# Softmax sums in an attention and feed-forward kernel: partial sums carried on over key tiles by GpSimd and VectorE, and one block of ones-matmuls for each pair of heads

## The chip, the core and the metric

The kernel runs on one core of one Trainium2 chip. A core has five engines that work side by side, each on its own queue in order: TensorE (PE, with its weight loads PEld), VectorE (DVE), ScalarE (ACT), GpSimd (POOL) and SyncE (SP), which here issues all transfers. The metric is the device time of one execution in microseconds (us); lower is better.

## What is computed

```python
def _attn_ref(q, k, v):                      # (8, 8, 1152, 64) each, float32
    B, H, S, D = q.shape
    scale = 1.0 / np.sqrt(D)
    q_pool = q.reshape(B, H, S // 2, 2, D).mean(axis=3)
    scores = scale * np.matmul(q_pool, k.transpose(0, 1, 3, 2))
    scores = scores - np.max(scores, axis=-1, keepdims=True)
    attn = np.exp(scores)
    attn = attn / (np.sum(attn, axis=-1, keepdims=True) + 1e-09)
    return np.matmul(attn, v).astype(np.float32)

def _moe_ref(x, w_in, w_out):                # (4608, 512), (512, 2048), (2048, 512)
    h = x @ w_in
    g = h - np.tanh(h)
    return (g @ w_out).astype(np.float32)
```

The output of the attention, 8 x 576 tokens with 8 heads of 64 values, is the `x` of the second function. The change is about `np.sum(attn)`, the softmax sums.

## The kernel before

There are two stages. The attention stage works on 32 pairs (4 pairs of heads in each of 8 batches, `NP` = 4). A pair has 576 queries after pooling, taken in two halves of 288 (`HQ`), and 1152 keys in nine tiles of 128. The time of this stage is counted in units: a unit is the scores of one head, one half and one key tile. Six units (three key tiles, two heads) are a group (`G` = 6), three groups are a half, 36 units (`U`) a pair.

In a unit (`score_unit`, line 281) PE makes 128 x 288 scores in a `ps_s` buffer (three of them) with two matmuls, and ScalarE takes their exponentials into `p_f`, the attention weights before division. `p_f` has four buffers of one group each. Keys lie on the partitions there. The sum over keys is therefore a sum over partitions and over tiles, and it is made in two steps. First GpSimd adds the three key tiles of a group for both heads at once, two adds of 128 x 576 (`z_part`, line 296). Then PE multiplies the result with a block of ones, 128 x 32, which sums over the partitions (`z_sums`, line 322).

Beside that, PE multiplies the weights with the values (`pv`, line 302: six fp32 matmuls a group, two heads in two halves of the array's columns, into `ps_o`), and it makes a first pass over the scores of later pairs to find their row maxima (`max_part`, line 241: matmuls into one of two `ps_m` buffers, each read by a VectorE reduction into `mx`, 14 a pair). VectorE also splits keys and queries into high and low parts (`kq_l`, line 215) and does most of the work on the weights of the second stage (`w`, `w_block`, line 371: one block every 34 units, to which GpSimd adds two instructions and ScalarE two). GpSimd also adds up the two pooled queries (`kq`, line 203).

What stands in which order is written out by hand. `add(u, f)` queues a step at a unit, and the loop at line 480 runs the steps of each unit; `InOrder` (line 27) keeps that order on every engine in this stage. The product of group n with the values comes five units after the group's last scores. The division comes later: the product is copied to `o_s` and stored unscaled in `x_dram`, the sums are copied to `z_s` and stored in `z_dram`; once a batch, `sums` (line 352) loads them as `rec`, VectorE takes reciprocals (line 361), and `spread` (line 366) stores them in `r_dram`. The maxima travel through `m_dram` and come back as two rows of the score operand (`there` and `back`, lines 270 and 273).

The second stage, the feed-forward part, takes 512 tokens at a time (`hidden`, line 522, and `second`, line 547); it loads `x_f` from `x_dram` and the reciprocals `x_r` from `r_dram` (line 96), and the multiplication of the first chunk happens on VectorE in the last units of the attention stage. In this stage a scheduler sets the order.

In the kernel before, a half has three partial sums, one of each group, in tiles `z` with four buffers. The block of ones-matmuls runs once for each half, after the first group of the next half: six matmuls of 288 columns, two heads and three groups. Each fills 32 columns of the array; two groups go side by side into four places, the third is added on the first two. The two places of each head are added after the load (line 363).

Of the kernel before, what the change touches and what calls it, by code (L numbers as in the profile page):

```python
# [43 lines left out]
def kernel(  # L44
# [18 lines left out]
    P = 128  # L63
    B, NP, _, _, SQ = q.shape
# [10 lines left out]
    dram = ctx.enter_context(tc.tile_pool(name="scratch", bufs=1, space=DRAM))  # L75
# [9 lines left out]
    ones = const.tile([P, 32], F32, name="ones")  # L85
# [1 line left out]


    x_dram = dram.tile([NP, P, NTOK], F32, name="x_dram")
    z_dram = dram.tile([B, 2, 2, NP, SQ], F32, name="z_dram")  # L90
# [50 lines left out]
    with ExitStack() as actx:  # L141
# [13 lines left out]
        HQ = SQ // 2  # L155
# [3 lines left out]
        G = 6  # L159
# [20 lines left out]
        def add(u, f, *args, at=at):  # L180
            at.setdefault(u, []).append(lambda: f(*args))
# [4 lines left out]
        pairs = {}  # L186

        def load(pi):
            w = pairs[pi] = Pair()
            w.b, w.hp = divmod(pi, NP)  # L190
            w.i = pi % 2
# [99 lines left out]
        class Group:  # L291
            pass

        late = []

        def z_part(grp):

            z = grp.z = zp.tile([P, 2, HQ], F32, name="z")
            pool.tensor_tensor(z, grp.p[:, :, 0], grp.p[:, :, 1], op=ALU.add)
            pool.tensor_tensor(z, z, grp.p[:, :, 2], op=ALU.add)  # L300

        def pv(u, grp):

            w, hf = grp.w, grp.half
            if grp.g == 0:
                hf.o = ps_o.tile([P, 512], F32, name="ps_o")
                hf.zs = []
            for j in range(3):
                kt = 3 * grp.g + j
                for h in range(2):  # L310
                    pe.matmul(hf.o[64 * h:64 * h + 64, 0:HQ], w.v[:, h, kt], grp.p[:, h, j], start=(kt == 0),
                              stop=(kt == KT - 1), tile_position=(0, 64 * h))
            hf.zs.append(grp.z)
            if grp.g == 2:
                add(u + 1, o_out, w, hf, at=first)
                late.append((w, hf))
                if w is pairs.get(n_pair - 1) and hf.n == 1:
                    add(u + G, lambda: z_sums(u + G, *late.pop()))
            elif late:
# [12 lines left out]
        def o_out(w, hf):  # L332
            if hf.n == 0:
                w.o_s = sm.tile([P, SQ], F32, name="o_s")
                w.z_s = sm.tile([P, SQ], F32, name="z_s")
            act.activation(w.o_s[:, hf.n * HQ:(hf.n + 1) * HQ], hf.o[:, 0:HQ], AF.Copy)

        def z_out(u, w, hf, ps):

            act.activation(w.z_s[:, hf.n * HQ:(hf.n + 1) * HQ], ps[:, 0:HQ], AF.Copy)  # L340
            if hf.n == 1:
                def store():
                    sp.dma_start(x_dram[w.hp, :, w.b * SQ:(w.b + 1) * SQ], w.o_s)
                    sp.dma_start(z_dram[w.b].rearrange("r h a s -> (r h) a s")[:, w.hp], w.z_s[0:P:32])
                add(u + 2, store)
                if w.hp == NP - 1:
                    add(u + 6, lambda: tot.append((w.b, sums(w.b))))
                    if w.b < B - 1:
                        add(u + 22, lambda: reciprocals(dve, *tot[0]))
                        add(u + 25, lambda: spread(sp, *tot.pop(0)))  # L350

        def sums(b):

            n = NP * 2 * SQ // P
            t = rec.tile([P, 2, n], F32, name="rec")
            for r in range(2):
                for h in range(2):
                    sp.dma_start(t[h * 64:h * 64 + 64, r], z_dram[b, r, h].rearrange("a (x n) -> (a x) n", n=n))
            return t

        def reciprocals(eng, b, t):

            eng.scalar_tensor_tensor(t[:, 0], t[:, 0], 1e-9, t[:, 1], op0=ALU.add, op1=ALU.add)
            eng.reciprocal(t[:, 0], t[:, 0])

        def spread(dma, b, t):
            dma.dma_start(r_dram[b].rearrange("h a (x n) -> (h a x) n", n=SQ * NP * 2 // P), t[:, 0])

        WB = 512

# [109 lines left out]
        for u in range(end + 60):  # L480
            run(u, first)
            if u < end:
                pi, r = divmod(u, U)
                half, r = divmod(r, U // 2)
                g, r = divmod(r, G)
                h, j = divmod(r, 3)
                if r == 0:
                    grp = Group()
                    if g == 0:
                        grp.half = Group()  # L490
                        grp.half.n = half
                    else:
                        grp.half = groups[-1].half
                    grp.w, grp.g = pairs[pi], g
                    grp.p = pf.tile([P, 2, 3, HQ], F32, name="p_f")
                    groups.append(grp)
                score_unit(grp.w, half, h, 3 * g + j, grp.p[:, h, j])
                if r == G - 1:
                    add(u + 1, z_part, grp)
# [131 lines left out]
```

## Time and profile before

| | us |
|---|---|
| median of three runs | 1827.98 |
| lowest, highest run | 1825.22, 1828.62 |
| the profiled execution, its own time | 1825.99 |
| its span, first to last instruction | 1824.2 |
| attention stage in it | from 0 to about 1000 |

A row of the profile gives an engine, a line (most of the attention stage has the line of a helper, L37, so groups are told apart by the names of their tiles), an operation with output and inputs, a count, and times. `ps_s<-z,ones` are the ones-matmuls, `z<-p_f` and `z<-z,p_f` the adds of GpSimd, `ps_m` and `mx` the row maxima, `ps_s<-t` the scores, `ps_o<-p_f,v` the product with the values. An fp32 matmul leaves two records. An idle time "<-" names what ended it.

### The profile page before, as it was taken

Reading aid. Unit: us, or ns where it says so; the run is one execution under the profiler, and the core shown is the slowest. Engines: PE = TensorE matmul, PEld = TensorE weight load, DVE = VectorE, ACT = ScalarE, POOL = GpSimd, SP = SyncE. Lnnn points to the kernel's source line nnn. Section 1 sums busy time; section 2 is a strip of 40 time slices with the busy share of each in tenths; the row PEclk is TensorE's granted clock in tenths of the full one; section 3 lists DMA queues with packets and bytes.
Section 4 is the critical chain, followed back from the end, with each engine's and each line's share of the span. In section 5 each row is a group of like instructions: output and inputs, shape, how many; then the busy total and the mean of one; then the engine's idle time right before and its main releaser. Section 6 shows DMA issues by size and latency. Waiting matters only on the chain. (4 is left out here: it accounts for less than half of the span.)

```text
span 1824.2 us, 28257 instructions
## 1 busy us (share of the span) xinstructions
PE 1741.4 (95%) x9920; PEld 1306.6 (72%) x9920; DVE 1403.8 (77%) x1823; ACT 1084.0 (59%) x2473; POOL 1050.4 (58%) x756
## 2 busy tenths in 40 slices
PE   4999999999999989999998999999999999999998
PEld 3666666766676666666665777878787888788887
DVE  5776767677767777776741899988998899888897
ACT  2555555656565555555554655666666666666676
POOL 2666778777787767777864274353534444433433
PEclk9999999999999999999999999999999999999999
DMA  8767787878878676878763821020101010100000
GB/s 211 201 175 219 180 227 196 221 196 219 228 207 232 168 213 181 212 212 227 196 169 131 313 58 64 6 65 6 64 9 61 13 57 18 44 14 34 27 15 21
DMA packets 104141, 242.29 MB, mean 133 GB/s; under 512 B 18112, under 2 KB 43328, under 8 KB 104000
## 3 DMA queue, kind: packets, MB, share of 16 engines
q1 hardware_dynamic: 104000, 240.49, 47.7%
q8 instruction: 78, 1.28, 0.3%
q14 instruction: 63, 0.52, 0.1%
HBM read 109.64 MB, written 36.42 MB: 80 GB/s over the span
## 5 line engine op out<-in xcount | busy, mean ns | idle before, releaser
L37 DVE TENSOR_REDUCE mx<-ps_m 128x2 f32<-128x768 f32 x448 | 405.5, 924 | 258.2 <-PE ps_m L37 257.9
L37 ACT ACTIVATE p_f<-ps_s 128x288 f32<-128x288 f32 x1152 | 418.0, 411 | 193.6 <-PE ps_s L37 169.7
L37 PE MATMUL ps_s<-t 128*128 128x288 f32 (+1 forms) x2304 | 447.6, 313 | 15.1 <-ACT p_f L37 9.1
L544 POOL TENSOR_TENSOR g_lo<-g_s,g_hi 128x512 fp32r<-128x512 f32 (+1 forms) x160 | 209.2, 1308 | 414.3 <-ACT g_hi L543 360.0
L37 PEld LDWEIGHTS ps_s<-t 128*128 128x128 f32 (+1 forms) x2304 | 357.2, 191 | 120.0 <-issue 90.2
L37 POOL TENSOR_TENSOR z<-p_f 128x576 f32<-128x576 f32 x192 | 289.7, 1509 | 159.5 <-PE ps_s L37 112.0
L526 PE MATMUL ps_h<-x,wi 128*128 128x512 f32 (+1 forms) x1440 | 325.0, 370 | 1.4 <-DVE g_s L541 1.4
L37 PE MATMUL ps_o<-p_f,v 128*64 128x288 f32 x2304 | 325.7, 419 | 0.0
L37 POOL TENSOR_TENSOR z<-z,p_f 128x576 f32<-128x576 f32 x192 | 290.4, 1512 | 17.9 <-ACT p_f L37 3.2
L526 PEld LDWEIGHTS ps_h<-x,wi 128*128 128x128 f32 x1440 | 254.9, 188 | 53.4 <-ACT g_u L532 1.8
L551 PE MATMUL ps_o<-wo,g_hi 128*128 128x512 f32 x1008 | 275.7, 392 | 4.2 <-ACT g_hi L543 3.8
L37 PE MATMUL ps_m<-x,bd 128*128 128x384 f32 x864 | 237.7, 355 | 32.0 <-DVE mx L37 17.5
L37 PEld LDWEIGHTS ps_o<-p_f,v 128*64 128x64 f32 x2304 | 149.8, 138 | 114.8 <-issue 29.8
L551 PEld LDWEIGHTS ps_o<-wo,g_hi 128*128 128x128 f32 x1008 | 186.8, 188 | 46.3 <-ACT g_hi L543 7.4
L543 ACT ACTIVATE g_hi<-g_s 128x512 fp32r<-128x512 f32 (+1 forms) x160 | 94.3, 590 | 153.8 <-DVE g_s L542 151.5
L37 PEld LDWEIGHTS ps_m<-x,bd 128*128 128x128 f32 x864 | 143.5, 196 | 49.6 <-DVE mx L37 27.9
L539 DVE SCALAR_TENSOR_TENSOR g_w<-g_w,g_u 128x512 f32<-128x512 f32 (+1 forms) x160 | 172.6, 1079 | 0.0
L551 PE MATMUL ps_o<-wo,g_lo 128*128 128x512 f32 x504 | 160.1, 393 | 5.6 <-POOL g_lo L544 5.4
L532 ACT ACTIVATE g_u<-ps_h 128x512 f32<-128x512 f32 (+1 forms) x160 | 87.5, 547 | 119.5 <-PE ps_h L526 119.0
L542 DVE COPY_PREDICATED g_s<-g_m,g_t 128x512 f32<-128x512 int32 (+1 forms) x160 | 133.3, 833 | 14.7 <-DVE g_s L541 0.5
L540 DVE SCALAR_TENSOR_TENSOR g_w<-g_s,g_w 128x512 f32<-128x512 f32 (+1 forms) x160 | 129.3, 808 | 18.8 <-ACT g_s L534 2.2
L541 DVE SCALAR_TENSOR_TENSOR g_s<-g_s,g_w 128x512 f32<-128x512 f32 (+1 forms) x160 | 126.5, 790 | 17.0 <-ACT g_t L533 0.5
(60 smaller groups left out, 1887.8 us busy)
## 6 DMA issues: line engine op xcount, KB each, us to landing
t<-x SPq DMA_DIRECT2D x64, 432.0 KB
q_n<-in_q_dram SPq DMA_DIRECT2D x32, 576.0 KB
kq<-in_k_dram SPq DMA_DIRECT2D x32, 576.0 KB
t<-kq_l SPq DMA_DIRECT2D x64, 288.0 KB
t<-x SPq DMA_DIRECT2D x64, 288.0 KB
v<-in_v_dram SPq DMA_DIRECT2D x32, 576.0 KB
bd<-x SPq DMA_DIRECT2D x64, 144.0 KB
t<-kq_l SPq DMA_DIRECT2D x64, 144.0 KB
```

What stands on the lines that cost most here:

```text
L37: ins = self.tc.keep_in_program_order(f(*args, **kwargs))
L526: nc.tensor.matmul(h, wi[fc][:, w, c], x[:, c, 0:n], start=(j == 0), stop=(j == len(mm) - 1))
L532: nc.scalar.activation(u, h, AF.Square)
L539: nc.vector.scalar_tensor_tensor(w, w, PL, u, op0=ALU.mult, op1=ALU.mult)
L540: nc.vector.scalar_tensor_tensor(w, s2, P2, w, op0=ALU.add, op1=ALU.mult)
L541: nc.vector.scalar_tensor_tensor(s1, s1, P1, w, op0=ALU.add, op1=ALU.mult)
L542: last = nc.vector.copy_predicated(s1, m.bitcast(I32), th).ins
L543: nc.scalar.activation(g_h, s1, AF.Copy)
L544: nc.gpsimd.tensor_tensor(g_l, s1, g_h.bitcast(F32), op=ALU.subtract)
L551: nc.tensor.matmul(po[j], g[:, ts], wo[fc][:, w], start=(fc == 0 and i == 0), stop=(fc == NF - 1 and i == 2))
```

## The change

The partial sums are carried on. For each half, GpSimd adds the three tiles of the first group into `hf.z` and then adds the three tiles of the second group to it, three more adds. The third group gets a tile of its own, `z_2`, with two adds, and VectorE adds it to `hf.z`, ten units later. A half so has seven adds on GpSimd in place of six, and one on VectorE. `hf.z` has three buffers, `z_2` two.

The ones-matmuls run once for a pair, after the second group of the next pair, for both halves: four matmuls (two halves, two heads), each in its own 32 columns. Nothing is added up on PE. One copy to `z_s` then holds both halves, and two stores take it to `z_dram`, which has lost an axis; `sums` has one load where it had four, and the reciprocal adds only the constant. The product `x_dram` is stored by its own step, one unit after it is copied.

```diff
-        late = []
-
-        def z_part(grp):
-
-            z = grp.z = zp.tile([P, 2, HQ], F32, name="z")
-            pool.tensor_tensor(z, grp.p[:, :, 0], grp.p[:, :, 1], op=ALU.add)
-            pool.tensor_tensor(z, z, grp.p[:, :, 2], op=ALU.add)
+        def z_part(u, grp):
+
+            hf = grp.half
+            if grp.g < 2:
+                if grp.g == 0:
+                    hf.z = zp.tile([P, 2, HQ], F32, name="z", bufs=3)
+                    pool.tensor_tensor(hf.z, grp.p[:, :, 0], grp.p[:, :, 1], op=ALU.add)
+                for j in range(2 if grp.g == 0 else 0, 3):
+                    pool.tensor_tensor(hf.z, hf.z, grp.p[:, :, j], op=ALU.add)
+            else:
+                z = zp.tile([P, 2, HQ], F32, name="z_2", bufs=2)
+                pool.tensor_tensor(z, grp.p[:, :, 0], grp.p[:, :, 1], op=ALU.add)
+                pool.tensor_tensor(z, z, grp.p[:, :, 2], op=ALU.add)
+                add(u + 10, lambda: dve.tensor_tensor(hf.z, hf.z, z, op=ALU.add))
...
-            hf.zs.append(grp.z)
             if grp.g == 2:
-                add(u + 1, o_out, w, hf, at=first)
-                late.append((w, hf))
+                add(u + 1, o_out, u + 1, w, hf, at=first)
+                w.halves.append(hf)
                 if w is pairs.get(n_pair - 1) and hf.n == 1:
-                    add(u + G, lambda: z_sums(u + G, *late.pop()))
-            elif late:
-                z_sums(u, *late.pop())
+                    add(u + G, lambda: z_sums(u + G, w))
+            elif grp.g == 1 and hf.n == 0 and w.i_pair > 0:
+                z_sums(u, pairs[w.i_pair - 1])
 
-        def z_sums(u, w, hf):
+        def z_sums(u, w):
 
             ps = ps_s.tile([P, 512], F32, name="ps_s")
-            for g in range(3):
+            for hf in w.halves:
                 for h in range(2):
-                    r = 64 * (g % 2) + 32 * h
-                    pe.matmul(ps[r:r + 32, 0:HQ], ones, hf.zs[g][:, h], start=(g < 2), stop=(g > 0),
-                              tile_position=(0, r))
-            add(u + 1, z_out, u + 1, w, hf, ps, at=first)
+                    r = 64 * hf.n + 32 * h
+                    pe.matmul(ps[r:r + 32, 0:HQ], ones, hf.z[:, h], start=True, stop=True, tile_position=(0, r))
+            add(u + 1, z_out, u + 1, w, ps, at=first)
...
+        def z_out(u, w, ps):
+
+            z_s = sm.tile([P, HQ], F32, name="z_s")
+            act.activation(z_s, ps[:, 0:HQ], AF.Copy)
+
+            def store():
+                for i in range(2):
+                    sp.dma_start(z_dram[w.b, :, w.hp, i * HQ:(i + 1) * HQ], z_s[64 * i:64 * i + 64:32])
+            add(u + 2, store)
...
-            t = rec.tile([P, 2, n], F32, name="rec")
-            for r in range(2):
-                for h in range(2):
-                    sp.dma_start(t[h * 64:h * 64 + 64, r], z_dram[b, r, h].rearrange("a (x n) -> (a x) n", n=n))
+            t = rec.tile([P, n], F32, name="rec")
+            sp.dma_start(t, z_dram[b].rearrange("h a (x n) -> (h a x) n", n=n))
...
-            eng.scalar_tensor_tensor(t[:, 0], t[:, 0], 1e-9, t[:, 1], op0=ALU.add, op1=ALU.add)
-            eng.reciprocal(t[:, 0], t[:, 0])
+            eng.tensor_scalar(t, t, 1e-9, None, op0=ALU.add)
+            eng.reciprocal(t, t)
```

Where the instructions stand now is shown at three places. First PE, around the end of the first groups of a pair's two halves. Before, at the first group of a pair's second half or of the next pair alike:

```order
L37 MATMUL ps_s<-t_0_121 128x288
L37 MATMUL ps_s<-t_0_122 128x288
L37 MATMUL ps_o<-p_f,v 64x288 x6
L37 MATMUL ps_s<-z,ones 32x288 x6
L37 MATMUL ps_s<-t_0_121 128x288
L37 MATMUL ps_s<-t_0_122 128x288
L37 MATMUL ps_m<-x,bd_125 128x384 x2
```

Now, after the second group of a pair, for the pair ahead of it:

```order
L37 MATMUL ps_s<-t_0_121 128x288
L37 MATMUL ps_s<-t_0_122 128x288
L37 MATMUL ps_o<-p_f,v 64x288 x6
L37 MATMUL ps_s<-z,ones 32x288 x4
L37 MATMUL ps_s<-t_0_121 128x288
L37 MATMUL ps_s<-t_0_122 128x288
```

The block stands once a pair, one group later, with four matmuls; at the first groups the scores follow the product with the values directly.

Second VectorE, at the tenth unit of a pair, where the maxima of the next pair are gathered (`nm`, `m2`) and the first reductions of the pair after it follow (numbers behind a name tell buffers apart):

```order
L37 TENSOR_REDUCE nm_1357<-mx_812 128x5 x2
L37 CAST m2_1360<-nm_1357 128x10
L37 TENSOR_TENSOR m2_1360<-nm_1357,m2_1360 128x10
L37 TENSOR_TENSOR z_1170<-z_1170,z_2_1275 128x576
L37 TENSOR_REDUCE mx_1145<-ps_m_1387 128x2
L37 TENSOR_REDUCE mx_1145<-ps_m_1403 128x2
```

The `z` row is new, for the second half of the pair before; the reductions stand behind it. The add for a first half stands at the 28th unit, between reductions.

Third SyncE, at the end of a batch. Before:

```order
L37 DMA x_dram<-o_s 128x576
L37 DMA z_dram<-z_s 4x576
L37 DMA wi_dram<-w_hl 256x4x128
L37 DMA m_dram<-mt 2x10x128
L37 DMA rec<-z_dram 64x36 x4
L37 DMA t_1_124<-m_dram 2x2x576
L37 DMA bd_126<-x 64x576 x2
```

Now:

```order
L37 DMA m_dram<-mt 2x10x128
L37 DMA z_dram<-z_s 2x288 x2
L37 DMA t_1_124<-m_dram 2x2x576
L37 DMA rec<-z_dram 128x36
L37 DMA bd_126<-x 64x576 x2
```

The stores of the sums come behind the store of the maxima and ahead of their load; the store of `x_dram` has moved up.

More of the change, by code (lines that the diff above doesn't have):

```diff
@@ L89 @@
     x_dram = dram.tile([NP, P, NTOK], F32, name="x_dram")
-    z_dram = dram.tile([B, 2, 2, NP, SQ], F32, name="z_dram")
+    z_dram = dram.tile([B, 2, NP, SQ], F32, name="z_dram")
     r_dram = dram.tile([B, 2, NP, SQ], F32, name="r_dram")
@@ L190, in load @@
             w.b, w.hp = divmod(pi, NP)
-            w.i = pi % 2
+            w.i, w.i_pair, w.halves = pi % 2, pi, []
             w.t2 = t2[w.i]
@@ L306, in pv @@
                 hf.o = ps_o.tile([P, 512], F32, name="ps_o")
-                hf.zs = []
             for j in range(3):
@@ L332, in o_out @@
-        def o_out(w, hf):
+                    r = 64 * hf.n + 32 * h
+                    pe.matmul(ps[r:r + 32, 0:HQ], ones, hf.z[:, h], start=True, stop=True, tile_position=(0, r))
+            add(u + 1, z_out, u + 1, w, ps, at=first)
+        def o_out(u, w, hf):
             if hf.n == 0:
                 w.o_s = sm.tile([P, SQ], F32, name="o_s")
-                w.z_s = sm.tile([P, SQ], F32, name="z_s")
             act.activation(w.o_s[:, hf.n * HQ:(hf.n + 1) * HQ], hf.o[:, 0:HQ], AF.Copy)
-        def z_out(u, w, hf, ps):
-            act.activation(w.z_s[:, hf.n * HQ:(hf.n + 1) * HQ], ps[:, 0:HQ], AF.Copy)
@@ L341, in z_out @@
             if hf.n == 1:
[L342 to L350, printed above, removed]
+                add(u + 2, lambda: sp.dma_start(x_dram[w.hp, :, w.b * SQ:(w.b + 1) * SQ], w.o_s))
@@ new lines, in z_out @@
+        def z_out(u, w, ps):
[5 more added lines that the diff above has]
+            add(u + 2, store)
+            if w.hp == NP - 1:
+                add(u + 6, lambda: tot.append((w.b, sums(w.b))))
+                if w.b < B - 1:
+                    add(u + 22, lambda: reciprocals(dve, *tot[0]))
+                    add(u + 25, lambda: spread(sp, *tot.pop(0)))
@@ L364, in reciprocals @@
-            eng.reciprocal(t[:, 0], t[:, 0])
+            eng.tensor_scalar(t, t, 1e-9, None, op0=ALU.add)
+            eng.reciprocal(t, t)
         def spread(dma, b, t):
-            dma.dma_start(r_dram[b].rearrange("h a (x n) -> (h a x) n", n=SQ * NP * 2 // P), t[:, 0])
+            dma.dma_start(r_dram[b].rearrange("h a (x n) -> (h a x) n", n=SQ * NP * 2 // P), t)
         WB = 512
@@ L498 @@
                 if r == G - 1:
-                    add(u + 1, z_part, grp)
+                    add(u + 1, z_part, u + 1, grp)
             run(u)
```

## The prediction

> **What bounds the kernel now.** I first read the page's busy times, then the stretches, to find out where TensorE (PE) is the limit.
>
> ```profile
> span 1824.2 us, 28257 instructions
> PE 1741.4 (95%) x9920; PEld 1306.6 (72%) x9920; DVE 1403.8 (77%) x1823; ACT 1084.0 (59%) x2473; POOL 1050.4 (58%) x756
> ...
> 60.00:940.00 880.00, 849.28 (x5783) 592.80 (x5783) 633.89 (x789) 503.86 (x1356) 653.45 (x444) 0.99 0.77 205
> 940.00:1011.00 71.00, 63.55 (x386) 41.46 (x385) 11.92 (x22) 32.32 (x88) 34.80 (x25) 0.93 0.46 143
> 1100.00:1824.00 724.00, 708.32 (x3248) 580.82 (x3246) 636.71 (x862) 475.35 (x897) 291.64 (x235) 1.00 0.10 32
> ```
>
> The columns of a stretch are its length, then the busy time of PE, PEld, DVE, ACT and POOL. The change touches the attention stage only. There, from 60 to 940 us, PE is busy for 849.28 of 880 us (97%), GpSimd (POOL) for 74%, VectorE (DVE) for 72%. A busy share alone does not say that an engine sets the pace, so next come the waits of PE in that stretch (total, times, longest).
>
> ```profile
> PE ps_m L37 <- DVE mx L37: 21.1, 22, 1.9
> PE ps_s L37 <- ACT p_f L37: 5.4, 15, 0.9
> PE ps_m L37 <- ACT mt L37: 4.0, 23, 0.2
> ```
>
> PE waits 30.5 us in 880, two thirds of it for VectorE's maxima to give back a `ps_m` buffer. No transfer and no GpSimd instruction stands in the list. So PE's own work sets the pace of the attention stage, and time taken off PE is taken off the end, until one of its two neighbours with three quarters of their time used comes up to it. Both are given more work here.
>
> **What PE loses.** The block of ones-matmuls, by the timeline of PE (start, length, operation, count); the fourth row is a narrower look at the same block, which shows only its last four records.
>
> ```profile
> 523.05 1.68 PE L37 MATMUL ps_o<-p_f,v 128*64 128x288 f32 x12
> 524.65 1.16 PE L37 MATMUL ps_s<-z,ones 128*32 128x288 f32 x12
> 525.75 0.54 PE L37 MATMUL ps_s<-t 128*128 128x288 f32 x2
> 525.16 0.66 PE L37 MATMUL ps_s<-z,ones 128*32 128x288 f32 x4
> ...
> 519.19 1.68 PE L37 MATMUL ps_o<-p_f,v 128*64 128x288 f32 x12
> 520.80 0.40 PE L37 MATMUL ps_s<-t 128*128 128x288 f32 x1
> ```
>
> From the start of the block to the start of the next score matmul are 525.75 − 524.65 = 1.10 us. The `ps_o` block ahead of it takes 1.60 us from start to start when a z block follows (523.05 to 524.65) and 1.61 us when a score matmul does (519.19 to 520.80), so taking the z block out takes out its full 1.10 us and leaves no remnant. Each fp32 matmul leaves two records. Six matmuls run in four groups of 32 columns: eight records (four matmuls) start between 524.65 and 525.16, the last four (two matmuls, in the first two groups again) follow behind them at 525.16, and the next block begins 0.59 us after that. A block of four matmuls in four groups is one such round; I take 0.61 us for it (0.59 us, and 0.02 us for a first round that also fills: the first one took 0.51 us to the next start).
>
> Before there are 64 blocks (32 pairs of heads, two halves), 64 × 1.10 = 70.0 us at the unrounded 1.094 us. After there are 32 blocks, 32 × 0.61 = 19.5 us. PE loses 50.5 us, 0.79 us a half. The bounds are tight: if four matmuls cost four sixths of 1.10 us it would be 47 us, if only the records' round of 0.51 us, 54 us.
>
> **What VectorE and GpSimd gain, and what of it reaches PE.** The groups between 60 and 940 us (busy, mean ns | idle before), and smallest/median/largest duration of two tiles over the whole span.
>
> ```profile
> L37 DVE TENSOR_REDUCE mx<-ps_m 128x2 f32<-128x768 f32 x388 | 363.5, 953 | 235.3 <-PE ps_m L37 235.0
> L37 POOL TENSOR_TENSOR z<-p_f 128x576 f32<-128x576 f32 x177 | 268.6, 1518 | 136.3 <-PE ps_s L37 100.1 <-ACT p_f L37 35.6 <-issue 0.3
> L37 POOL TENSOR_TENSOR z<-z,p_f 128x576 f32<-128x576 f32 x177 | 268.1, 1515 | 16.3 <-ACT p_f L37 2.7
> L37 DVE TENSOR_TENSOR kq_l<-kq,x 128x576 fp32r<-128x576 f32 x87 | 97.2, 1117 | 0.0
> L37 DVE TENSOR_SCALAR w<-w 128x512 int32<-128x512 int32 x62 | 48.8, 787 | 0.0
> L37 DVE SCALAR_TENSOR_TENSOR w<-w,w 128x512 int32<-128x512 int32 x31 | 34.7, 1119 | 0.1
> L37 DVE SCALAR_TENSOR_TENSOR w<-w_raw,w 128x512 f32<-128x512 uint16 x31 | 27.5, 889 | 0.1
> L37 DVE TENSOR_SCALAR w<-w 128x512 f32<-128x512 f32 x31 | 24.2, 782 | 1.4 <-ACT w L37 1.4
> L37 ACT ACTIVATE z_s<-ps_s 128x288 f32<-128x288 f32 x59 | 24.2, 411 | 107.6 <-PE ps_s L37 107.6
> ...
> L37 POOL TENSOR_TENSOR z<-p_f x192: 1392/1417/1947, 41.0 to 988.5; 128x576 f32<-128x576 f32 x192
> L37 DVE TENSOR_TENSOR kq_l<-kq,x x96: 741/1096/1978, 6.2 to 910.1; 128x576 fp32r<-128x576 f32 x96
> ```
>
> VectorE's new add (64 of them) has the shape of `kq_l`: two operands in SBUF, 128x576. Its row gives 1.12 us on average, 1.98 at most: 72 to 127 us more on VectorE. What of that reaches PE has bounds of 0 (VectorE already waits 235 us for PE in this stretch, 4.0 us for each of 59 halves, more than an add takes) and 127 us (each add held PE for its whole length). The nearest rows decide between them: `kq_l` and the four kinds of `w` work come into the same queue between the same maxima, 97.2 + 48.8 + 34.7 + 27.5 + 24.2 = 232 us, and PE's wait for `mx` in the stretch is 21.1 us, 9% of it. At that share the adds cost PE 6.5 to 11.5 us; I take 8. Queued behind an add that waits for GpSimd are the maxima, for which PE waits at its next-but-one `ps_m`. The add is queued ten units after the group's sums; a group of six units takes about a sixth of a pair's 29.8 us (880 us / 29.5 pairs), so ten units are 8.3 us, while GpSimd needs 3.0 us for the two sums: a lag of some 5 us is free. In front of the ones-matmul the add has seven more units, 5.8 us.
>
> GpSimd: 64 more adds at 1.51 us (seven a half in place of six), 97 us; and a sum that runs into a two-operand instruction of VectorE has taken 1.95 in place of 1.42 us, so up to 0.53 us more for each VectorE add, 34 us. Neither lies on PE's path while GpSimd has room: zero on the sum, with the room counted under the rivals. What goes away is GpSimd's largest wait, the 100.1 us above for `ps_s`: a sum there waited for one of four `z` buffers until PE had multiplied an old one. Three carried sums are enough now, since PE frees two at once at the 17th unit of the next pair, before the fourth is needed.
>
> [...]
>
> ScalarE loses half of the `z_s` copies, 32 × 0.41 = 13 us, beside PE: nothing on the sum. SyncE issues two stores of `z_dram` a pair in place of one, and one load of `rec` a batch in place of four.
>
> ```profile
> 527.90 0.57 SPq L37 DMA_DIRECT2D z_dram<-z_s  x1
> ...
> 976.45 1.26 DVE L37 TENSOR_TENSOR x_f<-x_f,x_r 128x512 f32<-128x512 f32 x1 [32.20 <-DMA x_r<-r_dram]
> 1000.59 10.55 PE L526 MATMUL ps_h<-x,t 128*128 128x512 f32 x36 [4.73 <-ACT x L37]
> ```
>
> That is 32 × 0.57 = 18 us more and 24 × 0.57 = 14 us less over the stage. The stores now stand between the store of `m_dram` and its load back, at the 20th and 24th unit; that load is wanted at unit 36, ten us later, and two issues are 1.1 us. Nothing on the sum.
>
> At the end of the stage the last add stands on VectorE behind the products of the first chunk, which wait for `x_r` (above: VectorE 32 us, PE 4.73 us behind it). PE meets its last two ones-matmuls among the 36 matmuls of the first chunk; I put 1 us there, bounds 0 and 3. The feed-forward stage runs the same instructions in a somewhat different order in its first chunk: 0, with 3 us either way.
>
> **Sum.** The profiled execution took 1825.99 us (span 1824.2 and 1.8 around it). 1826.0 − 50.5 + 8 + 1 = 1784.5. The median of the three runs shown, 1827.98, lies 2.0 above the profiled one, so I forecast 1786 us.
>
> **Rivals.** GpSimd's waits between 60 and 940 us:
>
> ```profile
> POOL z L37 <- PE ps_s L37: 100.1, 44, 4.7
> POOL w L37 <- DVE w L37: 43.2, 18, 5.1
> POOL z L37 <- ACT p_f L37: 38.4, 57, 4.0
> POOL kq L37 <- DMA q_n<-in_q_dram: 26.8, 14, 5.0
> POOL w_hl L37 <- ACT w_hl L37: 3.3, 6, 1.1
> POOL w L37 <- ACT p_f L37: 1.3, 2, 0.6
> POOL z L37 <- issue: 0.3, 1, 0.3
> ```
>
> *GpSimd takes the pace (slower).* Its work in the stretch becomes 653.4 + 59 × 1.515 + 59 × 0.53 = 774 us. Without the first row it still has 113 us of waits for others and 13 us of small gaps. If all of these stay, because GpSimd works strictly in order and each wait holds the sums behind it, the 59 halves take 774 + 113 + 13 = 900 us: 20 longer than now, 22 over 64 halves, 1850 us. They decide for slower from 82% of them on (774 + 13 + 93 = 880). For it: in-order queue, two engines that now wait for each other (`w` for VectorE, the new add for GpSimd). Against it: a wait of an engine that is early shrinks when it comes later, and GpSimd has four `p_f` buffers of slack. With PE at 841 us (880 − 59 × 0.79 + 7) GpSimd can keep 47% of the 113 us and still not be met.
>
> *GpSimd takes the pace in part (still faster).* Three quarters of those waits stay: 774 + 13 + 85 = 872 us, 8.5 us gained over the stage, 1819 us; at six tenths (855 us), 1801.
>
> *The transfers hide it (no change).* If SyncE's queue or the DMA engines were the pace, PE's 50 us would turn into waits for operands, 1828 us. The DMA share of 0.77 would rise to 0.81, and PE's list of waits has no transfer in it; unlikely.
>
> The change does what it says: PE's queue has four ones-matmuls a pair where it had twelve.
>
> **How the numbers follow.** The forecast with its own range of 1775 to 1800 (47 or 54 us on PE, 3 to 20 us of new waits, 3 us of order) gets 0.72, GpSimd in part (1800 to 1825) 0.14, no change 0.03, GpSimd whole and slower 0.11. Within 0.2% (3.7 us) is about what a measurement of this kernel cannot tell from no change. Faster 0.86, same 0.03, slower 0.11. The range takes in the likeliest case and most of the second: 1774 to 1814.
>
> **What would show it.** Right: ones-matmuls 256 records at 32 blocks of 0.61 us; PE's wait for `mx` between 25 and 35 us; VectorE's adds at 1.1 to 1.5 us; GpSimd at 90% or more of the stage with no wait for `ps_s`. Wrong: a wait of VectorE's `z` for GpSimd of more than 20 us in all, PE waiting long for `mx` right behind it, or ScalarE's `p_f` waiting for GpSimd's sums. A feed-forward stage that moves by more than 3 us would also upset the sum.

## The result and the profile after

The changed kernel took 1842.03 us (median of 4 runs, 1837.24 to 1843.62), the kernel before 1828.30 us on the same chip (4 runs, 1825.22 to 1831.85). The ratio is 1.0079, with a 95% interval of 1.0062 to 1.0096: slower by about 14 us. The prediction of 1786 us was wrong in sign, and the time lies outside its range. The profiled execution took 1837.24 us, the lowest of the four, against 1825.99 before.

The page's busy times after, then the stretch from 60 to 940 us as before (length, then busy time of PE, PEld, DVE, ACT and POOL, the granted TensorE clock, the DMA share, GB/s):

```profile
span 1835.2 us, 27322 instructions
PE 1715.1 (93%) x9408; PEld 1299.5 (71%) x9408; DVE 1511.0 (82%) x1887; ACT 1077.4 (59%) x2441; POOL 1174.1 (64%) x820
```

```profile
60.00:940.00 880.00, 811.82 (x5216) 575.99 (x5218) 718.08 (x841) 490.18 (x1307) 755.15 (x493) 0.97 0.75 201
```

PE did lose work: its busy time over the span fell from 1741.4 to 1715.1 us. But in the stretch from 60 to 940 us it is now busy for 92% where it was busy for 97%, and its clock there fell from 0.99 to 0.97. VectorE rose from 72% to 82%, GpSimd from 74% to 86%. Neither is full, and no engine took PE's place as the bound. The work that went away left idle time.

The exponentials mark where the attention stage begins and ends (smallest, median and longest duration in ns, first and last start in us), before and after:

```profile
L37 ACT ACTIVATE p_f<-ps_s x1152: 382/410/453, 38.0 to 989.8; 128x288 f32<-128x288 f32 x192
```

```profile
L37 ACT ACTIVATE p_f<-ps_s x1152: 384/411/444, 39.0 to 1000.7; 128x288 f32<-128x288 f32 x192
```

From the last exponential to the end are 834.4 us before (1824.2 − 989.8) and 834.5 after (1835.2 − 1000.7). All of the 11.0 us by which the profiled span grew is in the attention stage; 1.0 us of it is there at the first exponential.

PE's waits from 60 to 940 us in the changed kernel (in all, times, longest), then span and mean granted clock of the kernel before and of the changed one:

```profile
PE ps_m L37 <- DVE mx L37: 53.1, 41, 3.8
PE ps_s L37 <- ACT p_f L37: 12.8, 17, 4.5
PE ps_m L37 <- ACT mt L37: 1.3, 7, 0.3
```

```profile
core 0: 1824.2 us, clock 0.994
```

```profile
core 0: 1835.2 us, clock 0.980
```

Three terms make the balance of the profiled executions:

| term | us |
|---|---|
| ones-matmuls, as forecast | −50.5 |
| PE's waits from 60 to 940 us, 30.5 before, 67.2 after | +36.7 |
| time lost to the clock, span × (1 − clock), 10.9 before, 36.7 after | +25.8 |
| sum | +12.0 |
| measured on the span | +11.0 |

The first term held: a block of four ones-matmuls (eight records) begins at 510.48 us and the next score matmul at 511.10, 0.62 us for the 0.61 assumed.

```profile
510.48 0.69 PE L37 MATMUL ps_s<-z,ones 128*32 128x288 f32 x8
511.10 0.81 PE L37 MATMUL ps_s<-t 128*128 128x288 f32 x4
```

**Where the waits stand.** The groups of the changed kernel from 60 to 940 us (busy, mean ns | idle before) put more than half of them at one instruction, the transpose of the maxima, which runs once a pair and had 5.1 us of idle time ahead of it before. The last row is that of the cast in the kernel before:

```profile
L37 PE MATMUL ps_m<-ident_r,m 128*20 128x128 f32 x29 | 7.0, 241 | 36.9 <-DVE mx L37 36.4
L37 DVE TENSOR_TENSOR z<-z,z 128x576 f32<-128x576 f32 x58 | 74.3, 1281 | 2.6 <-POOL z L37 2.6
L37 DVE TENSOR_SCALAR w<-w 128x512 int32<-128x512 int32 x62 | 55.4, 893 | 0.0
L37 DVE CAST m<-nm 128x10 fp32r<-128x10 f32 x29 | 26.4, 910 | 1.0
```

```profile
L37 DVE CAST m<-nm 128x10 fp32r<-128x10 f32 x29 | 23.5, 809 | 1.0
```

VectorE's add hardly waits for GpSimd (2.6 us in 58). It costs its own 1.28 us and stands in a crowded place. One such place, by the timeline of the changed kernel (start, length, engine, operation, count, idle before):

```profile
470.00 6.43 POOL L37 TENSOR_TENSOR z<-z,p_f 128x576 f32<-128x576 f32 x4
470.13 0.23 DVE L37 TENSOR_REDUCE nm<-mx 128x5 f32<-128x15 f32 x2
470.40 1.12 DVE L37 CAST m<-nm 128x10 fp32r<-128x10 f32 x1
471.55 0.17 DVE L37 TENSOR_TENSOR m<-nm,m 128x10 fp32r<-128x10 f32 x1
471.64 1.65 DVE L37 TENSOR_SCALAR w<-w 128x512 int32<-128x512 int32 x1
473.20 1.98 DVE L37 TENSOR_TENSOR z<-z,z 128x576 f32<-128x576 f32 x1
475.11 1.88 DVE L37 SCALAR_TENSOR_TENSOR w<-w,w 128x512 int32<-128x512 int32 x1
476.91 1.81 DVE L37 TENSOR_REDUCE mx<-ps_m 128x2 f32<-128x768 f32 x2
477.91 0.23 PE L37 MATMUL ps_m<-ident_r,m 128*20 128x128 f32 x1 [3.45 <-DVE mx L37]
```

The same place of the same pair in the kernel before:

```profile
465.42 0.23 DVE L37 TENSOR_REDUCE nm<-mx 128x5 f32<-128x15 f32 x2
465.68 0.17 DVE L37 CAST m<-nm 128x10 fp32r<-128x10 f32 x1
465.89 0.17 DVE L37 TENSOR_TENSOR m<-nm,m 128x10 fp32r<-128x10 f32 x1
465.97 0.42 DVE L37 TENSOR_SCALAR w<-w 128x512 int32<-128x512 int32 x1
466.43 0.69 DVE L37 SCALAR_TENSOR_TENSOR w<-w,w 128x512 int32<-128x512 int32 x1
466.57 1.16 PE L37 MATMUL ps_s<-z,ones 128*32 128x288 f32 x12
467.41 1.43 POOL L37 TENSOR_TENSOR z<-p_f 128x576 f32<-128x576 f32 x1 [2.20 <-PE ps_s L37]
468.60 1.84 DVE L37 TENSOR_REDUCE mx<-ps_m 128x2 f32<-128x768 f32 x2 [1.48 <-PE ps_m L37]
469.61 0.23 PE L37 MATMUL ps_m<-ident_r,m 128*20 128x128 f32 x1
```

Read the two side by side. Before, VectorE ran from the gathered maxima to the end of the `w` work in 1.7 us (465.42 to 467.12), then stood idle for 1.48 us until PE had made new maxima. After, the same work and the add take 6.9 us (470.13 to 476.99), and the reduction that gives PE its `ps_m` buffer comes last. Three things differ. The add itself is new (1.98 us). GpSimd runs four sums back to back for 6.43 us, where it had stood idle for 2.20 us waiting for a `z` buffer, and beside it VectorE's instructions are stretched: 0.17 to 1.12, 0.42 to 1.65, 0.69 to 1.88 us. And PE no longer has 1.1 us of ones-matmuls to run meanwhile.

This place shows the stretching at its strongest. Over the whole 880 us VectorE's instructions were stretched in the kernel before too, and the difference is smaller: the mean of the cast rose from 809 to 910 ns, that of the int32 `w` row from 787 to 893 ns.

**Where the clock goes.** Four stretches around that wait (columns as above):

```profile
470.70:474.40 3.70, 3.70 (x26) 2.58 (x24) 3.67 (x4) 1.76 (x5) 3.54 (x3) 1.00 0.99 206
474.40:478.00 3.60, 0.15 (x3) 0.09 (x2) 3.60 (x4) 0.41 (x1) 1.96 (x2) 1.00 0.94 289
478.50:481.90 3.40, 3.40 (x14) 2.15 (x15) 2.11 (x4) 0.82 (x2) 2.73 (x2) 0.50 0.64 262
482.00:486.00 4.00, 4.00 (x34) 2.85 (x30) 1.69 (x2) 2.38 (x7) 3.04 (x4) 1.00 0.07 13
```

PE is idle for 3.45 us, then runs for 3.4 us at a granted clock of 0.50, then at 1.00 again. The wait costs twice: 3.45 us, and 1.7 us of work not done in the 3.4 us behind it. Such a stretch lasts 3.41 or 6.83 us. Ahead of the last exponential there are 4 before the change (13.7 us) and 12 after it (64.9 us); half of the difference, 25.6 us, is nearly all of the clock term of the table (25.8).

### The profile page after: what moved, and what is told of

Same layout as the page of the kernel before. It is cut to its first block, busy times and chain, and to the rows that moved or that the text cites. A ratio compares the mean times of both kernels' runs of the same rounds, so it can differ in the third digit from the quotient of the medians.

```text
span 1835.2 us, 27322 instructions
## 1 busy us (share of the span) xinstructions
PE 1715.1 (93%) x9408; PEld 1299.5 (71%) x9408; DVE 1511.0 (82%) x1887; ACT 1077.4 (59%) x2441; POOL 1174.1 (64%) x820
## 3 DMA queue, kind: packets, MB, share of 16 engines
q8 instruction: 74, 1.21, 0.3%
## 5 line engine op out<-in xcount | busy, mean ns | idle before, releaser
L37 POOL TENSOR_TENSOR z<-z,p_f 128x576 f32<-128x576 f32 x320 | 502.5, 1570 | 40.1 <-ACT p_f L37 18.1
L37 PE MATMUL ps_s<-t 128*128 128x288 f32 (+1 forms) x2304 | 452.4, 316 | 22.2 <-ACT p_f L37 16.1
L37 PEld LDWEIGHTS ps_s<-t 128*128 128x128 f32 (+1 forms) x2304 | 362.6, 193 | 124.8 <-issue 77.0
L37 PE MATMUL ps_o<-p_f,v 128*64 128x288 f32 x2304 | 336.2, 429 | 0.0
L37 PE MATMUL ps_m<-x,bd 128*128 128x384 f32 x864 | 242.7, 362 | 31.0 <-DVE mx L37 18.2
L37 PEld LDWEIGHTS ps_o<-p_f,v 128*64 128x64 f32 x2304 | 153.6, 141 | 120.6 <-issue 38.7
L37 POOL TENSOR_TENSOR z<-p_f 128x576 f32<-128x576 f32 x128 | 199.6, 1559 | 32.1 <-ACT p_f L37 32.1
L546 DVE SCALAR_TENSOR_TENSOR g_s<-g_s,g_w 128x512 f32<-128x512 f32 (+1 forms) x160 | 121.2, 758 | 16.6
```

Source lines behind the costliest of these rows:

```text
L37: ins = self.tc.keep_in_program_order(f(*args, **kwargs))
L546: nc.vector.scalar_tensor_tensor(s1, s1, P1, w, op0=ALU.add, op1=ALU.mult)
```

## The experiments

Each is compared with the kernel before on the same chip, as a ratio with its 95% interval. Each diff is against the changed kernel, if no other is named. Differences between two kernels are taken between their ratios, times 1826 us; by the intervals they are good to about 4 us. Where waits or the clock are named, they are those of the one profiled execution.

**VectorE's add: left out, or later in the queue.**

```diff
 e1_no_add
-                add(u + 10, lambda: dve.tensor_tensor(hf.z, hf.z, z, op=ALU.add))
 e2_add_later
-                add(u + 10, lambda: dve.tensor_tensor(hf.z, hf.z, z, op=ALU.add))
+                add(u + (10, 16)[hf.n], lambda: dve.tensor_tensor(hf.z, hf.z, z, op=ALU.add))
```

> The VectorE add of the third group's sum is left out, so the sums miss the third group of each half; GpSimd still makes seven adds a half. Theory (VectorE's queue: the add, up to 2.0 us with the contention, stands in front of the maxima for which PE's transpose waits, and each such wait of 3 us is followed by 3.4 to 6.8 us at half the TensorE clock): the long waits at the transpose go, at most three half-clock stretches are left before 940 us, 1785 to 1798 us. Rival A (GpSimd's 64 more adds set the pace): no change against the changed kernel, 1838 to 1845 us. Rival B (the moved stores and loads make operands late): no change either, 1838 to 1845 us.

> Same work as the changed kernel; only the add of a pair's second half is queued sixteen units after its group in place of ten, behind the transpose of the maxima and not in front of it. Theory: PE's wait for VectorE at the transpose falls below 2 us each, the half-clock stretches at the 15th unit of pairs 13 to 20 go, 1800 to 1818 us. Rival A and rival B: within 4 us of the changed kernel's 1842 us. If the amount of VectorE work counts and not its place: 1835 us or more too.

e2_add_later also leaves out a little: in the very last pair the ones-matmul reads the second half's sum before the third group is added, so that half's sums lack a third.

Without the add: 1810.54 us, 0.9916 (0.9900 to 0.9933). With the second half's add six units later: 1815.76 us, 0.9938 (0.9917 to 0.9959). PE's wait for `mx` from 60 to 940 us, for e1_no_add and then e2_add_later:

```profile
PE ps_m L37 <- DVE mx L37: 31.4, 28, 3.0
```

```profile
PE ps_m L37 <- DVE mx L37: 37.6, 39, 3.0
```

VectorE's add costs 29.8 us (1.0079 − 0.9916), and 25.7 us of that (1.0079 − 0.9938) is bound to its place: moved behind the transpose, it costs 4, which the intervals do not tell from nothing. But e1_no_add is 12 us above the 1785 to 1798 expected, with nine half-clock stretches before 940 us where at most three were. e2_add_later's time came as expected, its waits did not: they still reach 3.0 us where less than 2 was expected, and six half-clock stretches still stand behind transposes between 430 and 630 us. The add is not all of it.

**GpSimd's adds: eight a half, or six.**

```diff
 e3_gpsimd_all
-            if grp.g < 2:
+            if grp.g < 3:
 e4_six_adds
-            if grp.g < 2:
...
+            z = zp.tile([P, 2, HQ], F32, name="z" if grp.g == 2 else "z_2", bufs=3)
+            pool.tensor_tensor(z, grp.p[:, :, 0], grp.p[:, :, 1], op=ALU.add)
+            pool.tensor_tensor(z, z, grp.p[:, :, 2], op=ALU.add)
+            hf.z = z
```

> GpSimd adds the third group to the carried sum itself: eight adds a half on GpSimd, none on VectorE. Theory: VectorE is relieved, the waits at the transpose are those of the kernel before, GpSimd is close to full (its adds alone 16 x 1.42 = 22.7 us a pair of 27 to 28 us), 1785 to 1810 us. Rival A: slower than the changed kernel, 1860 us or more. Rival B: 1838 to 1845 us.

> GpSimd makes six adds a half as in the kernel before, no add on VectorE, PE multiplies the third group's sum only, so the sums miss the first two groups; PE's ones-matmuls are those of the changed kernel. Theory: within 6 us of the kernel with seven adds and no VectorE add, about 1780 to 1792 us. Rival A: 30 us or more below that kernel. Rival B: 1838 us or more.

Eight adds: 1858.13 us, 1.0170 (1.0155 to 1.0185). Six: 1800.24 us, 0.9848 (0.9832 to 0.9863). Both theories missed: the first by 48 us, close to rival A, the second by 8 us. The stretch from 60 to 940 us of e3_gpsimd_all, PE's waits there, and two of ScalarE's:

```profile
60.00:940.00 880.00, 805.32 (x5109) 566.96 (x5110) 658.79 (x762) 478.61 (x1280) 804.40 (x539) 0.96 0.74 197
```

```profile
PE ps_m L37 <- DVE mx L37: 39.1, 32, 3.3
PE ps_s L37 <- ACT p_f L37: 31.2, 24, 3.8
```

```profile
ACT x L37 <- POOL kq L37: 25.7, 11, 5.1
ACT w_hl L37 <- POOL w L37: 24.2, 15, 3.4
```

With eight adds GpSimd is at 91% and PE waits for `p_f`. The exponentials come late because ScalarE, in order, first waits for GpSimd's `kq` and `w`, 50 us in all; no wait for a `p_f` buffer is in its list. That is GpSimd taking the pace, my first rival, but in this kernel and not in the changed one (86%; there these two waits of ScalarE are 2.7 and 4.3 us, beside 6.0 at one place told of below). From six adds to seven, GpSimd's 64 more cost 12.4 us (0.9916 − 0.9848, both without VectorE's add); I had put them at zero. And even e4_six_adds, which adds work to no engine, gains only 27.8 us of the 50.5 that PE is spared. Its PE waits are 44.5 us and its clock 0.986, 14.3 us more lost than before (1798.9 × 0.014 = 25.2, less 10.9). Ahead of the transpose alone it waits 16.2 us, against 5.1 before. So taking the z blocks away has a price of its own.

**The block's place, with two sums a half and no add on VectorE.**

```diff
 e5_two_parts
-                z = zp.tile([P, 2, HQ], F32, name="z_2", bufs=2)
+                z = zp.tile([P, 2, HQ], F32, name="z_2", bufs=3)
...
-                add(u + 10, lambda: dve.tensor_tensor(hf.z, hf.z, z, op=ALU.add))
+                hf.z2 = z
...
+            for i in range(2):
...
+                        pe.matmul(ps[r:r + 32, 0:HQ], ones, (hf.z, hf.z2)[i][:, h], start=(i == 0), stop=(i == 1),
+                                  tile_position=(0, r))
 e8_two_parts_early, against e5_two_parts
-            elif grp.g == 1 and hf.n == 0 and w.i_pair > 0:
+            elif grp.g == 0 and hf.n == 0 and w.i_pair > 0:
```

> No add on VectorE: PE adds the third group's sum itself, eight ones-matmuls a pair in two rounds of four (1.10 us in place of 0.61), GpSimd keeps its seven adds; the block stays behind the second group. Theory (VectorE's add costs 30 us, GpSimd's 10, PE's extra round 32 x 0.49 = 16 at most): the kernel without the add, 1810 us, plus up to 16, so 1814 to 1827 us and as many waits at the transpose as there. Rival (PE's time counts for little, since it waits anyway): 1808 to 1813 us.

> As the kernel with eight ones-matmuls a pair, but the block stands behind the first group of the next pair (11th unit), ahead of the transpose of the maxima, as one of the two blocks of the kernel before did. Theory of cover (the old block at the 11th unit gave VectorE 1.1 us in which PE did not wait): PE's waits at the transpose fall by 5 us or more and with them the half-clock stretches; 6 to 15 us below the kernel with the block at the 17th unit. Rival (place of the block does not matter): within 3 us of it.

At the 17th unit of a pair: 1819.59 us, 0.9956 (0.9940 to 0.9971). At the 11th, ahead of the transpose: 1808.02 us, 0.9890 (0.9873 to 0.9907). The same instructions, one block moved by six units, are worth 12 us (0.9956 − 0.9890). The waits ahead of the transpose, e5_two_parts first, then e8_two_parts_early:

```profile
L37 PE MATMUL ps_m<-ident_r,m 128*20 128x128 f32 x29 | 6.7, 232 | 20.8 <-DVE mx L37 20.8
```

```profile
L37 PE MATMUL ps_m<-ident_r,m 128*20 128x128 f32 x31 | 7.1, 229 | 7.6 <-DVE mx L37 7.6
```

The block is cover for VectorE's queue: while PE runs it, VectorE catches up. The half-clock stretches behind a transpose, which were to go with the waits, went from seven to four.

**Three sums a half, as before, in one early block.**

```diff
 e6_three_parts
...
+            z = zp.tile([P, 2, HQ], F32, name="z", bufs=8)
+            pool.tensor_tensor(z, grp.p[:, :, 0], grp.p[:, :, 1], op=ALU.add)
+            pool.tensor_tensor(z, z, grp.p[:, :, 2], op=ALU.add)
+            hf.zs = [z] if grp.g == 0 else hf.zs + [z]
...
-            elif grp.g == 1 and hf.n == 0 and w.i_pair > 0:
+            elif grp.g == 0 and hf.n == 0 and w.i_pair > 0:
...
+            for i in range(3):
...
+                        pe.matmul(ps[r:r + 32, 0:HQ], ones, hf.zs[i][:, h], start=(i == 0), stop=(i == 2),
+                                  tile_position=(0, r))
```

> GpSimd's six adds of the kernel before, no add on VectorE; the three sums of both halves go through one block of twelve ones-matmuls a pair (three rounds, about 1.58 us, in place of two blocks of 1.10 us), behind the first group of the next pair. PE saves 32 x (2.19 - 1.58) = 20 us and neither neighbour gets work. Theory: most of it arrives, 1805 to 1815 us against 1826. Rival (whatever shortens PE's queue comes back as waits for VectorE and half clock): 1816 to 1828 us.

1805.96 us, 0.9880 (0.9865 to 0.9894), as expected. Twelve ones-matmuls a pair on PE, no sum carried on, and it is 36 us faster than the changed kernel. PE waits 3.6 us ahead of the transpose, and there are three half-clock stretches ahead of the last exponential (four before). It has the stores and loads of the changed kernel and gains the full 20 us that PE is spared, so moving them cost nothing that shows here.

**PE filled ahead of the transpose.** The changed kernel with more work for PE: in the ten pairs in which such a wait was followed by half clock, two blocks of six ones-matmuls on a constant, 2.2 us a pair.

```diff
 e7_fill
+    fill = const.tile([P, 288], F32, name="fill")
+    nc.vector.memset(fill, 1.0)
...
             def turn():
+                for _ in range(2 if pi in (3, 4, 6, 14, 15, 17, 18, 19, 20, 21) else 0):
+                    ps = ps_s.tile([P, 512], F32, name="ps_s")
+                    for i in range(6):
+                        r = 32 * (i % 4)
+                        pe.matmul(ps[r:r + 32, 0:HQ], ones, fill, start=True, stop=True, tile_position=(0, r))
```

> The changed kernel with work added: ahead of the transpose of the maxima, in the ten pairs in which its profile shows a half-clock stretch right behind it, PE makes two blocks of six ones-matmuls on a constant, 2.2 us each time, 22 us of more work whose result nobody reads. Theory (the wait, not the work, brings the half clock): the waits at these ten transposes shrink by about 2 us each, their half-clock stretches go, and the kernel gets faster by 8 to 25 us in spite of the work: 1817 to 1834 us. Rival (the half clock has another cause, such as the amount of work before it): stretches stay, 1842 us or more, up to 1864.

1830.52 us (10 runs), 1.0018 (1.0006 to 1.0031): with 22 us more PE work the kernel is 11 us faster (1.0079 − 1.0018). The place shown above, in this kernel, with the two stretches from the transpose on:

```profile
469.61 2.13 PE L37 MATMUL ps_s<-fill,ones 128*32 128x288 f32 x24
...
473.15 0.23 PE L37 MATMUL ps_m<-ident_r,m 128*20 128x128 f32 x1 [1.41 <-DVE mx L37]
```

```profile
473.10:476.50 3.40, 3.05 (x23) 1.81 (x27) 2.75 (x4) 1.09 (x3) 2.17 (x2) 1.00 0.90 361
476.60:480.00 3.40, 3.40 (x28) 2.69 (x22) 1.74 (x2) 2.43 (x7) 3.40 (x3) 1.00 0.08 22
```

The wait is 1.41 us in place of 3.45, and the clock behind it stays at 1.00. Of the ten filled transposes three still have half clock behind them, 3.4 us each. Ahead of the last exponential five half-clock stretches are left of twelve (20.5 us of 64.9), and the mean clock is 0.990. The half clock belongs to PE's idle time: only work on PE was added, and half clock became less.

**The transpose later.** From the third pair on the transpose is put off by three units and the store behind it by two, so that VectorE has had time for its queue: in the changed kernel, in e6_three_parts and in e8_two_parts_early.

```diff
 e9_turn_later, e10_three_parts_turn_later, e11_two_parts_turn_later
-            row, steps = -26, (5, 8, 14)
+            row, steps = -26, (8, 10, 14)
```

> The changed kernel, with no work added or taken away; only the transpose of the maxima stands eight units behind the start of its step in place of five, and the store behind it ten in place of eight, so that VectorE has 2.4 us more before PE needs it. Theory (the add, the gathering of the maxima and the weights' work stand in VectorE's queue ahead of the reduction that frees the transpose's buffer): the waits at the transpose fall by half or more, the half-clock stretches at it go, 1808 to 1825 us. Rival (VectorE's or GpSimd's amount of work sets the pace, the place only shows it): the waits move to other matmuls, 1836 us or more.

> The kernel with one block of twelve ones-matmuls a pair, with the transpose three units later as well. Its waits at the transpose are only 3.6 us in all, so theory: little to gain, 1800 to 1807 us. Rival (the later transpose brings the maxima back too late for the scores): slower by 5 us or more, with PE waiting for the load of m_dram.

> Eight ones-matmuls a pair at the 11th unit, GpSimd's seven adds, no VectorE add, and the transpose three units later. Theory: the half-clock stretches at the transpose that are left in the kernel without this shift go, 1796 to 1806 us. Rival (GpSimd's 64 adds set the pace by now): no change, 1807 to 1812 us.

On the changed kernel: 1827.22 us (10 runs), 1.0001 (0.9987 to 1.0016). On three sums: 1791.34 us, 0.9810 (0.9793 to 0.9827). On two sums: 1798.19 us, 0.9844 (0.9823 to 0.9864). PE's wait for `mx` from 60 to 940 us, e9_turn_later first, then all its waits there in e10_three_parts_turn_later, and that kernel's clock:

```profile
PE ps_m L37 <- DVE mx L37: 48.5, 39, 3.8
```

```profile
PE ps_m L37 <- DVE mx L37: 16.3, 18, 1.5
PE ps_s L37 <- ACT p_f L37: 6.8, 18, 1.0
```

```profile
core 0: 1788.3 us, clock 0.996
```

e9_turn_later missed its 1808 to 1825 by 2 us. The waits at the transpose did go, but they moved: the next maxima matmul that wants a `ps_m` buffer waits up to 3.8 us, as the rival had it, and the clock of the profiled execution stays at 0.980. So it isn't the transpose that is late, it is VectorE, and whatever PE wants next is what waits. Even so the edit is worth 14 us there (1.0079 − 1.0001), 13 on three sums (0.9880 − 0.9810) and 8 on two (0.9890 − 0.9844), so it pays with VectorE's add and without. On two sums that was expected, and no half-clock stretch is left behind a transpose. On three sums little had been expected (1800 to 1807 us); the waits fell by 4.9 us (28.0 to 23.1) and the clock's loss by 2, and what the other half of the gain is stays open.

e10_three_parts_turn_later beats both kernels. It takes the change's one block a pair, in place of two, and none of its carried sums. In its profiled execution the span is 35.9 us shorter than before. The ones-matmuls account for 21.3 of these (from the groups of 60 to 940 us, before and there: 68.7 us for 59 blocks, 1.164 × 64 = 74.5; 51.5 us for 31 blocks, 1.66 × 32 = 53.2), PE's waits for 7.4 (30.5 to 23.1), the clock for 3.7 (10.9 to 7.2).

```profile
L37 PE MATMUL ps_s<-z,ones 128*32 128x288 f32 x708 | 68.7, 414 | 0.0
```

```profile
L37 PE MATMUL ps_s<-z,ones 128*32 128x288 f32 x744 | 51.5, 410 | 0.0
```

The other 3.5 us stay open.

## Why the prediction was wrong

**What bounds the kernel.** That PE sets the pace of the attention stage was right before (97%), and after it is still the fullest engine there (92%, GpSimd 86%). That "time taken off PE is taken off the end, until one of its two neighbours with three quarters of their time used comes up to it" was not. No neighbour came up to it as a whole stage. VectorE came up to it for some 7 us, at one place in some of the pairs, and the full share of a stretch of 880 us doesn't show that.

**PE's own loss, −50.5 us.** Right (0.62 us a block). "Leaves no remnant" was right of the block's length and wrong of its place: e4_six_adds returns 22.7 us of the 50.5 although nothing was added, and moving the block by six units is worth 12 us. In the z block at a pair's 11th unit VectorE got through its queue: without it there, PE's waits ahead of the transpose are 16.2 to 21.6 us (e4_six_adds, e5_two_parts, e1_no_add), with it 3.6 to 7.6 (e6_three_parts, e8_two_parts_early; 5.1 before).

**VectorE's adds, "At that share the adds cost PE 6.5 to 11.5 us; I take 8".** This step failed most: 29.8 us by e1_no_add, inside the bounds of 0 and 127 and far from the value taken. I took the share of VectorE's two-operand work that PE waited for on average, 9%, and applied it to instructions that come at one place. The add of a pair's second half is queued ten units after its sums, which is between the gathering of maxima and the reduction that frees `ps_m`. I had named this reduction as queued behind the add, and priced only the add's wait for GpSimd (2.6 us in 58 adds, as free as I said), not its own length there. e2_add_later shows that 25.7 of the 29.8 us are this place.

**GpSimd's adds, "zero on the sum while it has room".** 12.4 us by e1_no_add and e4_six_adds. GpSimd did have room (86%, not the 90% I gave as the sign). It cost PE time all the same. By which way is not settled: from e4_six_adds to e1_no_add PE's waits grow at both ends, from 16.2 to 21.6 us ahead of the transpose, where VectorE is late, and from 11.2 to 15.2 us for `p_f`. "What goes away is GpSimd's largest wait", 100.1 us, was counted as room; the wait did go, and at the place shown it had been the time in which VectorE ran at full speed.

**The clock.** It was no term of the sum, though it is in the windows I quoted: 0.99 before. It takes 25.8 us, more than a third of all that was given back (62.5 us). The waits would have left 14 us of gain; with the clock it is a loss.

By the runs the sum is −50.5 for PE, +22.7 that come back when the z blocks go (e4_six_adds), +12.4 for GpSimd's adds, +29.8 for VectorE's: +14.4 us, which is 1.0079. That it closes is no proof, since the last three are differences from one kernel to the next and the 22.7 us are what was left of the 50.5. Since each of the three was measured with the half clock that follows its waits, the clock is in them. How the 22.7 us divide was not tried alone; the 12 us of the block's place is a share of it in another kernel, and some 6 us of it stand at the load of `q_n` below.

**The rest.** GpSimd taking the pace, the first rival, had the right sign and nearly the right time for another reason; it is the cause in e3_gpsimd_all. Of the signs named ahead, the long wait of PE for `mx` came (53.1 us, up to 3.8), though not behind a wait of VectorE's add for GpSimd.

Transfers were not the cause, with one exception: from 418 to 424 us GpSimd waits 7.47 us for a load of `q_n`, ScalarE's next copy can start only when GpSimd's `kq` ends (5.98 us idle), PE waits 4.5 us and runs 6.8 us at half clock, some 8 us in all. The same place is there without VectorE's add: in e1_no_add GpSimd waits 8.40 and PE 5.07 us, in e4_six_adds 8.54 and 2.90 us, with 3.4 and 6.8 us at half clock behind. So it is no part of the price of VectorE's add. In e6_three_parts GpSimd waits 5.68 and PE 0.87 us; before, GpSimd waited 4.97 us and PE not at all. Why the load comes later was not tried.

The time from the last exponential on moved by 0.1 us. The feed-forward stage held as forecast, and the 1 us put at the end of the attention stage is not seen there.

## What to carry to other kernels

Work on the pacing engine may be what hides a neighbour's queue: before it is removed, read the neighbour's queue at that very place, in order, with the durations it has beside the third engine, since a share over the whole stage says nothing there. Price a wait of PE at its length and the half-clock time behind it (from 45 us on, 3.4 to 6.8 us at 0.50 behind every wait of 1.9 us and more in the changed kernel), and keep the work that fills such a hole, or move it there. An idle engine can be paying for another: a buffer wait of GpSimd may not be room, where VectorE runs unstretched during it (0.42 and 0.69 us for two `w` instructions in GpSimd's 2.20 us at the place shown, 1.65 and 1.88 us beside its sums in the changed kernel).

## What the runs showed of the hardware

The clock fell behind waits of less than 2 us. From 45 us on (its records begin at 42.5 and 45.0 us), waits of PE of 1.28, 1.62 and 1.86 us in the kernel before were each followed by 3.4 us at 0.50, and others of 1.26 to 1.52 us were not; in the changed kernel every wait of 1.9 us and more was followed by 3.4 to 6.8 us at 0.50, and of the waits from 1.3 to 1.75 us only some.

What sorts these waits is how much of one falls into one step of a grid. In the traces of both kernels the half-clock stretches begin on a grid of 3.413 us: in the changed kernel at 423.92, 444.40 and 478.53 us, 6 and then 10 steps apart. Where PE was idle for at least 2.0 us of one such step at full clock, the next step was at 0.50 in all 8 cases; below 1.2 us it never was, in 490; between them it was in 6 of 11. (Idle time by PE's records, steps from 45 to 950 us of the two kernels.) The most idle time without half clock behind it was 1.35 us, the least with it 1.50 us. A wait that straddles two steps can so be longer and go free: the 1.75 us from 81.50 us on in the changed kernel, 1.08 us of it in one step and 0.67 in the next.

Beside GpSimd's instructions VectorE's small ones were stretched as much as its large ones. Over the span of the changed kernel (smallest, median and longest ns):

```profile
L37 DVE CAST m<-nm x32: 173/1000/1387, 26.1 to 955.8; 128x10 fp32r<-128x10 f32 x32
L37 DVE TENSOR_TENSOR z<-z,z x64: 743/950/2000, 62.6 to 1011.8; 128x576 f32<-128x576 f32 x64
```

The cast of ten elements in each partition had a median of 1.00 us there (0.90 in the kernel before) and took up to 1.39 us, 1.21 more than its shortest; the `z` add took up to 2.00, 1.26 more. From 60 to 940 us of the two kernels, the five casts with no GpSimd instruction beside them all took 0.17 us, and the 43 `w` rows of one operand (TENSOR_SCALAR) without one 0.36 to 0.43 us, against up to 1.69 beside one. Not every kind is stretched: the reduction `nm<-mx` took 150 to 171 ns in both kernels, beside GpSimd or not. What sets the kinds apart no run shows.
